# A state attention with two feed-forward nets: first two chunks in four ranges, parts added by the transfer, another opening order

## The chip, the cores and the metric

The kernel runs on one core of a Trainium2 chip. The metric is device microseconds of one execution; the numbers below are the median of several runs and one profiled execution. The engines are TensorE (PE), VectorE (DVE), ScalarE (ACT), GpSimd (POOL) and SyncE (SP), each with an in-order queue of its own; SP mostly issues transfers.

## The reference

Eight batches of an attention between tokens and a small state, then two feed-forward nets over all 4352 rows. The weights are float64, x and state float32.

```python
def _attn_ref(x, state):                       # x (8, 8, 512, 64), state (8, 8, 32, 64)
    scores = scale * np.matmul(x, state.transpose(0, 1, 3, 2))
    a = softmax(scores)                        # written out with max, exp and sum
    xread = np.matmul(a, state)
    scores2 = scale * np.matmul(state, x.transpose(0, 1, 3, 2))
    a2 = softmax(scores2)
    sread = np.matmul(a2, x)
    return np.concatenate([xread, sread], axis=2)

x = attn_out.transpose(0, 2, 1, 3).reshape(B * (S + Ns), 512)
h = np.maximum(x @ w_in, 0.0)                  # w_in 512 x 2048
y = h * h @ w_out                              # w_out 2048 x 512
out = ((y @ w1) * (y @ w2) @ w3) @ w_out2      # 512 x 1024, 512 x 1024, 1024 x 1024, 1024 x 512
```

## The kernel before

Everything is transposed: the 128 partitions hold features, the columns tokens. A *chunk* c is the 512 tokens of one batch (c = 0 to 7); chunk 8 is the 256 state rows of all batches. Products keep fp32 accuracy by splitting each operand into a high and a low half (`split`, L80: ScalarE casts the high half, VectorE subtracts it from the source, line L85, for the low one) and making three passes.

*First net.* For chunk c and each of 16 blocks f of 128 hidden features, `h_tile` (L417) makes six products from `SW` (state times w_in) and `aT` (the softmax), `act_h` (L409) takes relu and square and splits into `ghl`; `y_tile` (L452) makes twelve products of `ghl` with the split w_out (`wo`) into four PSUM banks, one for each d of 128 output features. The main loop (L604 on) runs over (c, f); `y_tile` follows `h_tile` by two tiles. Chunks 0 and 1 alternate in three ranges of f (0 to 4, 4 to 8, 8 to 16, `segs` at L91), so that weights are needed later; each range leaves a partial y per chunk, which is copied by ScalarE (even d) or VectorE (odd d) into one of two `yo` buffers and written to a DRAM scratch of its own by SP. For chunks 2 to 8 there is one range.

*Weights.* They arrive as float64 in pieces of 128 x 512 (three `raw` buffers). `convert64` (L124) makes fp32 by integer arithmetic: VectorE masks the exponent (L136), ScalarE rebases it (L137), VectorE masks the mantissa (L138) and has three more instructions (L141, L144, L147). `make_wout` then has ScalarE cast the high half and GpSimd subtract for the low half (L177). `conv` takes the next conversion of a list and issues the load of the third one after it; `side` and `late` say at which tile i which job is issued. The weights of the second net are converted the same way, later, and parked in DRAM.

*Opening.* SP issues state, x and w_in transfers in program order (L494 on); state goes out as eight small transfers. ScalarE or VectorE copies x of chunk 0 into another layout, GpSimd that of chunks 1 and 2. Then come transposes, scores, softmax, the first `SW` and the first hidden tile.

*Second net.* Pairs of chunks; `load_pair` (L718) reads the parts of y back, and for chunks 0 and 1 GpSimd adds them up.

The order on each engine is set by a scheduler from program order and its own estimates; `issue_after` keeps a job behind a named instruction.

## Time and profile before

| | |
|---|---|
| median of 3 runs | 1298.33 us (1297.55 to 1402.79) |
| the profiled execution | 1299.79 us |
| its span | 1298.0 us |
| busy: TensorE, VectorE, ScalarE, GpSimd | 97%, 62%, 50%, 4% of the span |
| mean granted TensorE clock | 0.988 |

The span is the profiled stretch on the core. A line number in a row is that of kernel.py; a helper such as L85 serves many callers, so the tile's name tells which. In a timeline row stand the start, the duration, engine, line, operation, and in brackets how long the engine had been idle before and what released it. Busy time of TensorE overstates its work, since products are pipelined and their rows overlap.

### The profile page before, as it was taken

Reading aid. Unit: us, or ns where it says so; the run is one execution under the profiler, and the core shown is the slowest. Engines: PE = TensorE matmul, PEld = TensorE weight load, DVE = VectorE, ACT = ScalarE, POOL = GpSimd, SP = SyncE. Lnnn points to the kernel's source line nnn. Section 1 sums busy time; section 2 is a strip of 40 time slices with the busy share of each in tenths; the row PEclk is TensorE's granted clock in tenths of the full one; section 3 lists DMA queues with packets and bytes.
Section 4 is the critical chain, followed back from the end, with each engine's and each line's share of the span. In section 5 each row is a group of like instructions: output and inputs, shape, how many; then the busy total and the mean of one; then the engine's idle time right before and its main releaser. Section 6 shows DMA issues by size and latency. Waiting matters only on the chain.

```text
span 1298.0 us, 16933 instructions
## 1 busy us (share of the span) xinstructions
PE 1255.5 (97%) x6392; PEld 988.4 (76%) x6392; DVE 801.2 (62%) x1428; ACT 651.6 (50%) x1170; POOL 57.4 (4%) x42
## 2 busy tenths in 40 slices
PE   3998999999999999999999999999999999999998
PEld 2575667777777777777789888888888888778877
DVE  6889966767666676733244763747464646566652
ACT  4675765656666575655465542535353542424231
POOL 0122300000000000000000000000510000000000
PEclk8898999999999999999999999999999999999999
DMA  6146626336353633400132432031631425050323
GB/s 210 53 145 199 188 61 179 126 82 186 79 159 97 152 125 81 139 1 28 31 119 82 138 115 75 29 101 43 185 103 44 137 75 158 37 193 19 113 65 98
DMA packets 122962, 137.95 MB, mean 106 GB/s; under 512 B 71424, under 2 KB 75008, under 8 KB 122368
## 3 DMA queue, kind: packets, MB, share of 16 engines
q1 hardware_dynamic: 122880, 136.87, 34.8%
q8 instruction: 50, 0.82, 0.3%
q14 instruction: 32, 0.26, 0.1%
HBM read 93.32 MB, written 43.52 MB: 105 GB/s over the span
## 4 chain that ended last, share of the span: by engine, by line
PE 83%; DVE 8%; DMA 4%; ACT 3%; issue 1%; SPq 0%; POOL 0%; DVEq 0%; ACTq 0%; POOLq 0%
PE y L461 24%; PE po L850 12%; PE qa L769 10%; PE qd L769 6%; PE ps_w L654 3%; PE qc L769 3%; PE qe L769 3%; PE ps_sw L396 2%; PE ab L824 2%; PE ps_r L345 1%; DMA out_dram<-o 1%; DMA x<-in_x_dram 1%; DVE ghl L85 1%; DVE sw L85 1%; DMA yscr<-yo 1%
## 5 line engine op out<-in xcount | busy, mean ns | idle before, releaser
L461 PE MATMUL y<-ghl,wo 128*128 128x512 f32 (+1 forms) x1728 | 408.5, 383 | 8.9 <-ACT yo L470 7.7
L461 PEld LDWEIGHTS y<-ghl,wo 128*128 128x128 f32 x1728 | 309.6, 189 | 101.1 <-ACT r L411 17.6
L85 DVE TENSOR_TENSOR ghl<-r,ghl 128x512 fp32r<-128x512 f32 (+1 forms) x144 | 97.1, 674 | 174.5 <-ACT ghl L84 173.9
L769 PE MATMUL qa<-yq,wq 128*128 128x512 f32 x576 | 146.3, 390 | 1.8 <-ACT s L777 1.8
L769 PEld LDWEIGHTS qa<-yq,wq 128*128 128x128 f32 x576 | 107.6, 188 | 25.9 <-ACT s L777 2.9
L777 ACT COPY s<-qa 128x512 f32<-128x512 f32 x96 | 56.1, 587 | 140.9 <-PE qa L769 128.9
L769 PE MATMUL qd<-yq,wq 128*128 128x512 f32 x384 | 98.3, 390 | 0.0
L850 PE MATMUL po<-w34b,c 128*128 128x512 f32 x408 | 95.8, 391 | 0.3 <-DVE o L859 0.3
L850 PE MATMUL po<-w,c 128*128 128x512 f32 x408 | 95.3, 391 | 0.0
L850 PEld LDWEIGHTS po<-w34b,c 128*128 128x128 f32 x408 | 75.7, 188 | 18.0 <-DVE c L85 1.0
L413 ACT ACTIVATE r<-r 128x512 f32<-128x512 f32 (+1 forms) x144 | 87.5, 608 | 2.9
L850 PEld LDWEIGHTS po<-w,c 128*128 128x128 f32 x408 | 75.6, 188 | 17.4 <-ACT c L84 0.8
L84 ACT CAST ghl<-r 128x512 fp32r<-128x512 f32 (+1 forms) x144 | 86.0, 597 | 5.1 <-PE y L461 1.6
L769 PEld LDWEIGHTS qd<-yq,wq 128*128 128x128 f32 x384 | 71.8, 188 | 15.7 <-ACT s L777 1.0
L137 ACT ACTIVATE ce<-ce,ebias 128x512 int32<-128x512 int32 x72 | 51.7, 722 | 44.3 <-DVE ce L136 44.2
L781 DVE TENSOR_TENSOR s<-qa,s 128x512 f32<-128x512 f32 x32 | 22.1, 692 | 75.5 <-ACT s L777 75.5
L84 ACT CAST c<-s 128x512 fp32r<-128x512 f32 x64 | 39.6, 621 | 35.6 <-DVE s L798 35.1
L727 POOL TENSOR_TENSOR yraw<-yraw,yp 128x512 f32<-128x512 f32 x16 | 21.8, 1362 | 760.5 <-DMA oscr<-o 745.6
L84 ACT CAST yq<-yraw 128x512 fp32r<-128x512 f32 x70 | 42.6, 622 | 24.1 <-DVE yraw L744 15.4
L144 DVE SCALAR_TENSOR_TENSOR ce<-raw,ce 128x512 int32<-128x512 int32 x72 | 50.3, 699 | 4.1 <-ACT ce L137 4.0
L859 DVE TENSOR_TENSOR o<-po,opart 128x512 f32<-128x512 f32 x34 | 23.4, 690 | 46.4 <-PE po L850 35.9
L141 DVE SCALAR_TENSOR_TENSOR cm<-raw,cm 128x512 f32<-128x512 uint32 x72 | 49.9, 693 | 0.8
(549 smaller groups left out, 1862.0 us busy)
## 6 DMA issues: line engine op xcount, KB each, us to landing
raw<-in_moe_w_dram SPq DMA_DIRECT2D x32, 512.0 KB, 4.4
yraw<-yscr SPq DMA_DIRECT2D x56, 256.0 KB, 5.4
raw<-in_moe_w_out_dram SPq DMA_DIRECT2D x24, 512.0 KB, 3.9
yscr<-yo SPq DMA_DIRECT2D x48, 256.0 KB, 2.5
oscr<-o SPq DMA_DIRECT2D x34, 256.0 KB, 2.2
opart<-oscr SPq DMA_DIRECT2D x34, 256.0 KB, 3.2
out_dram<-o SPq DMA_DIRECT2D x32, 256.0 KB, 2.9
raw<-in_moe_w_in_dram SPq DMA_DIRECT2D x12, 512.0 KB, 4.3
```

What stands on the lines that cost most here:

```text
L84: nc.scalar.copy(hi, src)
L85: return nc.vector.tensor_tensor(out=lo, in0=src, in1=f32(hi), op=ALU.subtract)
L137: nc.scalar.activation(e, e, ACTF.Relu, bias=ebias, scale=8.0)
L141: nc.vector.scalar_tensor_tensor(out=f32(m), in0=lw, scalar=2.0**-32, in1=m, op0=ALU.mult, op1=ALU.add)
L144: nc.vector.scalar_tensor_tensor(out=e, in0=hw, scalar=-(2**31), in1=e, op0=ALU.bitwise_and, op1=ALU.bitwise_or)
L396: nc.tensor.matmul(pss[r][k * NS:(k + 1) * NS, cols], stT[rows, b, k, :], win_t[fg][rows, k, cols], start=True, stop=True, tile_position=( ...
L413: nc.scalar.activation(r[:, :n], r[:, :n], ACTF.Square)
L461: nc.tensor.matmul(y_ps[c, d][:, :n], wo_t[f][:, wi, d * P:(d + 1) * P], t[:, gi, :n], start=(f == f0 and k == 0), stop=(f == f1 - 1 and k ...
L654: nc.tensor.matmul(ps, t[:, wi, (j % 4) * P:(j % 4 + 1) * P], wo2_t[j][:, vi, :], start=(j == 0 and k == 0), stop=(j == N1 - 1 and k == 2),)
L769: nc.tensor.matmul(ps, W[w, kt][:, wi, m * P:(m + 1) * P], Y[v, kt][:, vi, :], start=(first and kt == 0 and k == 0), stop=(last and kt == ...
L777: nc.scalar.copy(t, ps)
L850: nc.tensor.matmul(ps, v[:, vi, t * P:(t + 1) * P], w[:, wi, :], start=(m == 0 and k == 0), stop=(m == QM - 1 and k == 2),)
```

## The change

- Chunks 0 and 1 alternate in four ranges of four f each. There is one y scratch for each chunk: the first range is written by SP as before, the later three are added to it in memory by transfers with `accum_op=add`, which GpSimd issues. `load_pair` reads one y and adds nothing.
- `make_wout` no longer uses GpSimd: the split is the common one, on ScalarE and VectorE, and it is put off to the next `conv` (or to the first `y_tile` that needs it).
- `exponents` masks and rebases the exponents of the next piece already while a piece is converted.
- State's first half is issued from ScalarE's queue; both x pieces of chunk 0 go ahead of w_in, x of chunk 1 ahead of state's second half. ScalarE copies x of chunks 1 and 2. Both w_in conversions of the first columns and both softmax halves are issued before the first `aT`; the jobs of tile 0 are issued after the last `aT` of the opening.
- One `conv` for each tile from 7 to 25 (two at 10) in place of 7 to 22 (two at every fourth); the conversions for the second net begin at tile 32 in place of 24.

```diff
-    segs = [[(0, 4), (4, 8), (8, NF)] if c < 2 else [(0, NF)] for c in range(B + 1)]
+    segs = [[(f, f + 4) for f in range(0, NF, 4)] if c < 2 else [(0, NF)] for c in range(B + 1)]
+    y_scr = [dram.tile([P, ND, 512 if c < B else NT9], F32, name=f"yscr{c}") for c in range(B + 1)]
...
+    def exponents(key, t):
+        e = att.tile([P, 512], I32, tag="ce", bufs=2, name="ce")
+        nc.vector.tensor_single_scalar(e, t[:, :, 1], 0x7FF00000, op=ALU.bitwise_and)
+        nc.scalar.activation(e, e, ACTF.Relu, bias=ebias, scale=8.0)
+        exps[key] = e
...
     def make_wout(f):
         w = att.tile([P, 512], F32, tag="cw", bufs=2, name="cw")
         convert64(("wo", f), w)
-        t = wpool.tile([P, 2, DM], F32R, tag="wo", bufs=NF, name=f"wo{f}")
-        nc.scalar.copy(t[:, HI], w)
-        nc.gpsimd.tensor_tensor(out=t[:, LO], in0=w, in1=f32(t[:, HI]), op=ALU.subtract)
-        wo_t[f] = t
+
+        def halves():
+            t = wpool.tile([P, 2, DM], F32R, tag="wo", bufs=NF, name=f"wo{f}")
+            split(t[:, HI], t[:, LO], w)
+            wo_t[f] = t
+
+        open_splits.append(halves)
...
-                nc.sync.dma_start(y_scr[c][part][:, d, :], o[:, :n])
+                if part:
+                    nc.gpsimd.dma_start(y_scr[c][:, d, :], o[:, :n], accum_op=ALU.add)
+                else:
+                    nc.sync.dma_start(y_scr[c][:, d, :], o[:, :n])
...
     load_st(0)
     load_x(0, 0, True)
+    load_x(0, 1, True)
     load_win0(0, 0, True)
-    load_x(0, 1, True)
     make_x(0, 0, nc.vector)
     make_x(0, 1, nc.scalar)
     load_win0(0, 1, True)
-    load_wout(0, True)
     load_win0(1, 0, True)
     load_win0(1, 1, True)
+    load_wout(0, True)
+    for g in range(G):
+        load_x(1, g, True)
     load_st(1)
     for g in range(G):
-        load_x(1, g, True)
-    for g in range(G):
-        make_x(1, g, nc.gpsimd, True)
+        make_x(1, g, nc.scalar, True)
...
     def conv():
+        close_splits()
+        k, k1 = (convs[i] if i < len(convs) else None for i in (pos[1], pos[1] + 1))
         pos[1] += 1
+        if k and k not in exps:
+            exponents(k, raws[k])
+        if k1:
+            exponents(k1, raws[k1])
...
-    for i in range(7, 23):
-        side[i] = [conv] * (2 if i % 4 == 2 else 1)
+    for i in range(7, 26):
+        side[i] = [conv] * (2 if i == 10 else 1)
...
-                nc.sync.dma_start(t[:, n], y_scr[c][0][:, d, :])
-                for part in y_scr[c][1:]:
-                    p = bp.tile([P, 512], F32, tag="pt", bufs=2, name="yp")
-                    nc.sync.dma_start(p, part[:, d, :])
-                    nc.gpsimd.tensor_tensor(out=t[:, n], in0=t[:, n], in1=p, op=ALU.add)
+                nc.sync.dma_start(t[:, n], y_scr[c][:, d, :])
```

The order on SP's queue at the start, before:

```order
L482 DMA st_114<-in_state_dram 32x4x64 x8
L205 DMA x_0_123<-in_x_dram 128x4x256
L119 DMA raw<-in_moe_w_in_dram 128x512 x2
L205 DMA x_1_128<-in_x_dram 128x4x256
L119 DMA raw<-in_moe_w_in_dram 128x512 x2
L121 DMA raw<-in_moe_w_out_dram 128x1024
L119 DMA raw<-in_moe_w_in_dram 128x512 x4
L482 DMA st_145<-in_state_dram 32x4x64 x8
L205 DMA x_0_154<-in_x_dram 128x4x256
L205 DMA x_1_156<-in_x_dram 128x4x256
```

and in the change (x_0_119 and x_1_121 are chunk 0's, x_0_141 and x_1_143 chunk 1's):

```order
L118 DMA raw<-in_moe_w_out_dram 128x1024
L219 DMA x_0_119<-in_x_dram 128x4x256
L219 DMA x_1_121<-in_x_dram 128x4x256
L116 DMA raw<-in_moe_w_in_dram 128x512 x8
L118 DMA raw<-in_moe_w_out_dram 128x1024
L219 DMA x_0_141<-in_x_dram 128x4x256
L219 DMA x_1_143<-in_x_dram 128x4x256
L501 DMA st_145<-in_state_dram 32x4x64 x8
```

State's first half has left this queue, a w_out piece has moved to its head, and x of chunk 1 now stands ahead of the eight small transfers.

VectorE in the first softmax, before, from the maximum of its first half on (`win_210` is w_in, `e_219` the softmax half):

```order
L307 TENSOR_REDUCE mx<-ps_n 128x16
L141 SCALAR_TENSOR_TENSOR cm<-raw,cm 128x512
L308 TENSOR_TENSOR e_219<-ps_n,mx 128x512
L144 SCALAR_TENSOR_TENSOR ce<-raw,ce 128x512
L284 TENSOR_REDUCE nm<-S 128x1
L315 TENSOR_REDUCE sm_229<-e_219 128x16
L147 SCALAR_TENSOR_TENSOR win_210<-cm,ce 128x2x256
L316 TENSOR_SCALAR sm_229<-sm_229 128x16
```

and the same stretch in the change:

```order
L321 TENSOR_REDUCE mx<-ps_n 128x16 x2
L322 TENSOR_TENSOR e_223<-ps_n,mx 128x512
L322 TENSOR_TENSOR e_232<-ps_n,mx 128x512
L329 TENSOR_REDUCE sm_242<-e_223 128x16
L330 TENSOR_SCALAR sm_242<-sm_242 128x16
L331 RECIPROCAL sm_242<-sm_242 128x16
L332 TENSOR_TENSOR e_223<-e_223,sm_242 128x512
L329 TENSOR_REDUCE sm_256<-e_232 128x16
```

The conversions of w_in no longer stand between the steps of the softmax, and the second half (`e_232`) follows the first at once.

VectorE at the end of chunk 0's second part in the change, between the copies of d = 1 (`y_1040`) and d = 3 (`y_1042`), and what follows:

```order
L484 COPY yo<-y_1040 128x512
L125 TENSOR_SCALAR ce<-raw 128x512
L143 TENSOR_SCALAR cm<-raw 128x512
L85 TENSOR_TENSOR ghl<-r,ghl 128x512
L125 TENSOR_SCALAR ce<-raw 128x512
L146 SCALAR_TENSOR_TENSOR cm<-raw,cm 128x512
L149 SCALAR_TENSOR_TENSOR ce<-raw,ce 128x512
L484 COPY yo<-y_1042 128x512
L152 SCALAR_TENSOR_TENSOR cw<-cm,ce 128x512
L85 TENSOR_TENSOR sw_1206<-ps_sw,sw_1206 128x512
L85 TENSOR_TENSOR sw_1209<-ps_sw,sw_1209 128x512
L85 TENSOR_TENSOR wo_1241<-cw,wo_1241 128x512
```

The copy of d = 3 needs the buffer that the transfer of d = 1 empties; the last row is a low half of w_out, which stood on GpSimd before.

## Rows read from the trace of the kernel before

**Rows 1.** The page's first part: busy us, share, instructions.

```profile
PE 1255.5 (97%) x6392; PEld 988.4 (76%) x6392; DVE 801.2 (62%) x1428; ACT 651.6 (50%) x1170; POOL 57.4 (4%) x42
```

**Rows 2.** Stretches: length, busy by engine, PEclk, DMA share, GB/s.

```profile
46.00:100.00 54.00, 53.17 (x318) 35.76 (x316) 47.88 (x99) 39.03 (x72) 12.39 (x7) 1.00 0.38 122
100.00:125.00 25.00, 19.84 (x88) 14.70 (x86) 22.80 (x39) 13.96 (x25) 5.11 (x4) 0.86 0.60 190
125.00:160.00 35.00, 33.04 (x169) 23.93 (x170) 33.70 (x60) 24.54 (x44) 10.46 (x6) 1.00 0.62 189
...
300.00:700.00 400.00, 398.68 (x2179) 306.97 (x2178) 227.52 (x432) 235.35 (x420) 0.00 (x0) 1.00 0.34 94
```

**Rows 3.** Timeline around 160 us: VectorE, ScalarE and TensorE.

```profile
160.17 0.68 DVE L85 TENSOR_TENSOR ghl<-r,ghl 128x512 fp32r<-128x512 f32 x1
...
163.15 0.62 ACT L176 CAST wo<-cw 128x512 fp32r<-128x512 f32 x1 [2.57 <-DVE cw L147]
...
164.31 2.44 PE L396 MATMUL ps_sw<-win,stT 64*32 64x512 f32 x16 [3.46 <-ACT S L279]
```

**Rows 4.** Timeline of VectorE at 134 us.

```profile
134.37 0.68 DVE L144 SCALAR_TENSOR_TENSOR ce<-raw,ce 128x512 int32<-128x512 int32 x1
134.97 0.41 DVE L136 TENSOR_SCALAR ce<-raw 128x512 int32<-128x512 int32 x1
135.31 0.68 DVE L147 SCALAR_TENSOR_TENSOR win<-cm,ce 128x512 f32<-128x512 f32 x1
```

**Rows 5.** Timeline of the opening: TensorE, then VectorE.

```profile
27.24 1.08 PE L328 MATMUL ps_a<-ident,e 128*128 128x128 f32 x4 [7.55 <-DVE rs L291]
...
38.71 0.68 DVE L85 TENSOR_TENSOR aT<-ps_a,aT 128x512 fp32r<-128x512 f32 x1
```

**Rows 6.** Two more stretches, columns as in rows 2.

```profile
10.00:15.00 5.00, 2.13 (x11) 1.73 (x10) 3.29 (x7) 2.84 (x4) 0.00 (x0) 1.00 1.03 385
...
160.00:180.00 20.00, 16.55 (x80) 11.77 (x79) 11.80 (x24) 12.71 (x25) 3.18 (x2) 0.91 0.28 91
```

**Rows 7.** VectorE's groups from 40 to 165 us: busy us, mean ns, idle before.

```profile
L144 DVE SCALAR_TENSOR_TENSOR ce<-raw,ce 128x512 int32<-128x512 int32 x27 | 19.5, 724 | 1.5 <-ACT ce L137 1.4
L141 DVE SCALAR_TENSOR_TENSOR cm<-raw,cm 128x512 f32<-128x512 uint32 x26 | 18.6, 715 | 0.1
L85 DVE TENSOR_TENSOR ghl<-r,ghl 128x512 fp32r<-128x512 f32 x21 | 16.6, 792 | 1.3 <-ACT ghl L84 1.3
L147 DVE SCALAR_TENSOR_TENSOR cw<-cm,ce 128x512 f32<-128x512 f32 x15 | 13.1, 871 | 1.4 <-POOL wo L177 1.2
...
L147 DVE SCALAR_TENSOR_TENSOR win<-cm,ce 128x512 f32<-128x512 f32 x12 | 9.1, 761 | 0.0
```

**Rows 8.** The same groups from 210 to 700 us.

```profile
L85 DVE TENSOR_TENSOR ghl<-r,ghl 128x512 fp32r<-128x512 f32 x101 | 69.5, 688 | 160.3 <-ACT ghl L84 160.3
...
L147 DVE SCALAR_TENSOR_TENSOR cw<-cm,ce 128x512 f32<-128x512 f32 x37 | 25.4, 686 | 0.5
L144 DVE SCALAR_TENSOR_TENSOR ce<-raw,ce 128x512 int32<-128x512 int32 x37 | 25.3, 684 | 0.1
```

**Rows 9.** VectorE's waits from 40 to 165 us: total, times, longest.

```profile
DVE ce L144 <- ACT ce L137: 1.4, 1, 1.4
...
DVE yo L468 <- DMA yscr<-yo: 1.2, 2, 1.0
DVE cw L147 <- POOL wo L177: 1.2, 1, 1.2
```

**Rows 10.** Transfers: writes of a part (60 to 240 us), reads of one.

```profile
DMA to landing us min/median/max: 2.0/3.1/5.8
...
yp<-yscr SPq DMA_DIRECT2D x16, 256.0 KB, 3.3
```

**Rows 11.** The chain at 370 us: start, us, what.

```profile
370.04 1.36 PE ph__3529 L425 x6
371.40 2.72 PE y L461 x12
```

49 lines of the change are left out of this document (26 added, 23 removed).

## The prediction

> **What bounds it now.** I read the page's busy times first: TensorE is busy 97% of the span [rows 1], so what can be gained is the time in which it waits or computes at half clock. The table of stretches says where that is. From 300 to 700 us it is busy 398.7 of 400 us and VectorE 227.5: nothing to gain there. Between 46 and 160 us it is the other way round: VectorE is busy 47.9 of 54, 22.8 of 25 and 33.7 of 35 us, so it stands idle for 9.6 us of 114 [rows 2]. The weights arrive as 64-bit floats and VectorE turns each 512 KB piece into fp32 by five instructions; while that lasts, VectorE sets the pace and TensorE waits for it, often inside rows that count as busy. Where the lateness shows, the wait is named after another engine: at 163.15 ScalarE starts a cast that had waited 2.57 us for VectorE's `cw`; the two copies of `S` queue behind that cast, and TensorE waits 3.46 us for `S` [rows 3].
>
> So the account is kept on VectorE: its time to a fixed point is the work that stands ahead of that point in its own order, plus its waits, plus what its instructions take too long. A long instruction (128x512, 0.68 us) costs 0.60 us from start to start, a short one (0.41 us) 0.34 us [rows 4]. The point is the low half of the 21st hidden tile (`ghl`, L85), which starts at 160.17 [rows 3]. Counted in the two programs' orders, 157 long and 68 short instructions stand ahead of it before (94.2 + 23.1 = 117.3 us) and 160 long and 62 short in the change (96.0 + 21.1 = 117.1 us); the tiny ones are 34 in both. That is no accident of counting: twelve low halves of w_out come over from GpSimd (12 x 0.60 = 7.2 us), and three conversions of 2.5 us each have moved behind the point, since four ranges want the last weights later. The work is equal, so only waits and slow instructions change.
>
> **The change part by part.**
>
> *Opening, -4.0 us on VectorE.* Before, TensorE stands 7.55 us before the first transpose of the softmax at 27.24, and the low half of chunk 0's second `aT` starts at 38.71 [rows 5], ending near 39.3, with 27 long and 14 short instructions done by then (21.0 us): VectorE is 18.3 us late. In the change both x pieces of chunk 0 come before w_in, the state goes out from ScalarE's queue beside them, and both softmax halves run ahead of the second half of w_in. Ahead of x for chunk 1 lie 5.25 MB (state 0.25, two w_out pieces 1.0, x 1.0, w_in 2.0, x itself 1.0); the opening has reached 385 GB/s [rows 6], 13.6 us for all of it; with some 2 us to the first byte and 1.3 us to issue and land the last, its two pieces land near 15.6 and 16.9 us. I estimate ScalarE's two copies of them to end at 16.6 and 19.0, the second exponential behind them at 19.7, the second normalised half at 21.2, and the same low half of `aT` at 25.7, with 16 long and 6 short instructions done (11.6 us): 14.1 us late. That is 4.2 us less; I keep 4.0, for four tiny instructions fewer. TensorE's first hidden tile comes some 14 us earlier, but from there VectorE paces it. Bounds: 0 if chunk 1's x lands 4 us later, since ScalarE's exponential queues behind its copy; 7 if it lands 3 us sooner.
>
> *GpSimd does no arithmetic any more, -7.8 us.* Beside it VectorE's instructions were slow. From 40 to 165 us against 210 to 700 us, where GpSimd is idle, the means are: `ghl` 792 for 688 ns (21 of them, 2.2 us), `cw` 871 for 686 (15, 2.8 us), the same step on `win` 761 for 686 (12, 0.9 us), L144 724 for 684 (27, 1.1 us) and its like L141 715 (26, 0.8 us) [rows 7, 8]. Sum 7.8 us. Bounds: 7.8 is the measured excess of five groups; it falls to 3.9 if GpSimd, which now prepares the accumulating transfers in this stage, disturbs half as much by that.
>
> *Exponents one conversion ahead, -2.6 us.* VectorE waited 1.4 us for ScalarE's exponent and 1.2 us for GpSimd to free `cw` [rows 9]. Both causes go. A raw piece must now have landed one step sooner; yet in the order the work between the freeing of a raw buffer and the reading of its next content stays at 4 us at least and about 6 mostly in both programs, so the waits for raw data stay as they are.
>
> *Accumulating transfers, +2.2 us ahead of the point.* 24 transfers of 256 KB now add in memory, issued from GpSimd's queue. None is in the trace. The nearest row is the plain write of the same tile, 2.0 at least, 3.1 in the median, 5.8 at most; a read of the same part takes 3.3 [rows 10]. One that has to read and then write takes 3.1 at least and 3.3 + 3.1 = 6.4 if one follows the other; I take 4.5, nearer to the write, since reading and writing overlap along the lines of a transfer. Only two `yo` buffers exist, so the copy of d = 3 on VectorE waits for the transfer of d = 1. Between the two copies VectorE has three long and three short instructions, 2.8 us; it stands still for 4.5 - 2.8 = 1.7 us, and the conversions, `ghl` and casts behind it with it. Two such part ends lie ahead of the point: 3.4 us, less the 1.2 us that `yo` cost before [rows 9]. Bounds: -1.2 and +6.
>
> What the Trainium skill says of such transfers (DMA: Bandwidth & Descriptors, section "Anatomy of one DMA") would make it shorter: 2.0 us fixed plus bytes over 436 GB/s, an estimate of 2.6 us for these. By it VectorE would not wait at all and the forecast would be 1279 us. No run here shows it, and its fit is not for accumulation.
>
> *Behind the point, +1.4 us.* Between the 21st and the 24th `ghl` the change has 24 long and 7 short instructions, 16.8 us, where TensorE needs three tiles of 1.36 + 2.72 us [rows 11] and about 1.5 us of attention and `sw` products: 13.7. It loses 3.1 us, and one more part end costs VectorE 1.7 us: 4.8. Before, the same stretch lost the 3.45 us that TensorE is idle from 160 to 180 and 1.8 us by a granted clock of 0.91 [rows 6]: 5.2 us. So this is nearly even (-0.4). Three part ends are left after that, where VectorE has time again and TensorE itself is the one that would wait: it wants the bank of d = 2 again 5.4 us after a part's last tile begins (2.72 + 1.36 + 1.36), and the buffer needed for emptying it was filled at about 2.2 us: a cover of 3.2 us, or 4.3 where `sw` products stand between. Of 4.5 us that leaves 0.2 to 1.3; I take 0.6 for each, 1.8 in all, and so +1.4.
>
> *At no cost:* the 16 additions and 16 reads that fall away in the pair (0, 1) lie beside a TensorE that never waits for them; the stretch from 300 us on shows the same [rows 2]. ScalarE gets chunk 2's two x copies, about 1 us each, and would block if x were late; its margin is several tiles.
>
> **Sum.** -4.0 - 7.8 - 2.6 + 2.2 + 1.4 = -10.8 us. The profiled execution took 1299.8 us (span 1298.0); that gives 1289.0. The median of the runs, 1298.33, lies 1.5 us lower, so I say 1287, rounded down.
>
> **The rivals.**
>
> *A, VectorE lets go.* If the new order also removes the rest of VectorE's idle time (9.6 - 2.6 - 1.2 = 5.8 us) and part ends cost nothing (3.4 + 1.7 + 1.8), TensorE runs almost unhindered: 1287 - 12.7, about 1274, and with the upper bound of the opening, 3 us more, 1271. For it: the scheduler spreads the conversions evenly. Against it: idle time on a saturated VectorE came from many small causes that the change doesn't touch.
>
> *B, slow accumulation, the other side.* Each us above 4.5 costs 1 us at each of the six part ends, at three through VectorE and at three on TensorE itself: 6 us per us. The gain of 10.8 is gone at 6.3 us, where the kernel becomes slower than before; 6.4 us, read after write, gives 1298, 7 us give 1302. Slower by over 2% would need 10.7 us. For it: a plain write took up to 5.8 us [rows 10]. Against it: those stood behind loads in SP's queue, which these don't. The Trainium skill has a rule on this side too (SBUF — State Buffer, section "Who interferes with whom"): GpSimd cannot write descriptors while VectorE runs an instruction in its two-port mode. No run here shows it; VectorE's instructions of 0.41 us could hold it up, but none for long.
>
> *C, the opening doesn't get earlier.* If x for chunk 1 lands at 21 us or later, ScalarE's queue holds back the second softmax as GpSimd's did not: 1291 to 1295.
>
> **How the numbers follow.** The forecast has 0.53, with a range of its own of 1280 to 1294; A 0.23; B 0.16; C 0.08. The range 1268 to 1300 leaves out a tail of A and the upper half of B. About 2% is what a measurement of this kernel can tell from no change: faster than 1272.4 is most of A's lower half and a tail of the forecast, 0.16; slower than 1324.3 only a B of over 10 us, 0.04; the rest, 0.80, is within.
>
> **What would show it.** Right: the first hidden tile done near 26 us (41 before), no `ghl` or `cw` above 0.7 us, the 21st `ghl` near 148, VectorE still over 90% busy from 46 to 145 us. The accumulating transfers' time to landing decides between A and B. Wrong: VectorE with idle time in the middle while TensorE still waits, or waits for raw data that take over on VectorE.

## The result

The changed kernel takes 1307.84 us (median of 4 runs, 1306.15 to 1307.96) where the kernel before takes 1298.3: a ratio of 1.0072, 95% interval 1.0053 to 1.0092. It is 0.7% slower. The forecast was 1287, with 1300 as the upper end. The profiled execution took 1307.75 us, its span 1305.7.

The page's first part and the head of its chain, after (before: [rows 1]):

```profile
PE 1259.8 (96%) x6392; PEld 990.0 (76%) x6392; DVE 797.4 (61%) x1448; ACT 657.0 (50%) x1178; POOL 21.6 (2%) x30
...
PE 80%; issue 12%; ACT 3%; DVE 2%; DMA 2%; POOL 1%; ACTq 0%; SPq 0%; POOLq 0%; DVEq 0%
```

GpSimd has gone from 57.4 to 21.6 us and VectorE has lost a little, yet the span is longer. Where, the stretches say (columns as in [rows 2]):

```profile
46.00:100.00 54.00, 52.57 (x301) 36.06 (x294) 50.54 (x109) 38.71 (x70) 0.00 (x0) 1.00 0.41 132
100.00:125.00 25.00, 19.76 (x89) 14.24 (x88) 19.62 (x37) 15.54 (x25) 3.61 (x4) 0.96 0.77 206
125.00:160.00 35.00, 31.74 (x158) 23.33 (x158) 28.27 (x55) 21.52 (x38) 3.48 (x4) 0.93 0.66 147
160.00:210.00 50.00, 44.27 (x232) 32.15 (x231) 30.72 (x63) 28.07 (x53) 6.93 (x8) 0.93 0.67 115
210.00:250.00 40.00, 37.36 (x177) 25.18 (x177) 24.24 (x49) 22.10 (x39) 6.93 (x8) 0.96 0.64 110
300.00:700.00 400.00, 398.58 (x2145) 305.40 (x2145) 238.40 (x456) 237.53 (x420) 0.00 (x0) 1.00 0.37 106
```

Up to 100 us VectorE does more than before (50.5 of 54 us, 47.9 before). From 46 to 145 us it was to be busy over 90%; it is busy 84.7 of 99 us (before 90.5), and from 100 to 160 us 47.9 of 60 us (before 56.5). TensorE loses with it: 51.5 of 60 us from 100 to 160, then 81.6 of 90 from 160 to 250 us (before 52.9 and 85.6). From 300 us on nothing has changed. The mean granted clock is below full speed in all four stretches from 100 to 250 us. GpSimd's column is one row of 0.9 to 1.2 us for each accumulating transfer, four for each end of a part.

One such end, the first, in the timeline (the bracket is the idle time before and what ended it):

```profile
113.53 0.57 ACT L486 COPY yo<-y 128x512 f32<-128x512 f32 x1
...
114.42 1.01 POOL L488 DMA_DIRECT2D yscr<-yo  x1 [113.12 <-ACT yo L486]
...
114.87 0.68 DVE L484 COPY yo<-y 128x512 f32<-128x512 f32 x1
...
115.86 0.87 POOL L488 DMA_DIRECT2D yscr<-yo  x1 [0.43 <-DVE yo L484]
...
121.51 0.58 ACT L486 COPY yo<-y 128x512 f32<-128x512 f32 x1 [4.87 <-DMA yscr<-yo]
...
122.15 1.09 PE L477 MATMUL y<-ghl,wo 128*128 128x512 f32 x3 [4.51 <-ACT yo L486]
...
122.80 0.69 DVE L484 COPY yo<-y 128x512 f32<-128x512 f32 x1 [3.34 <-DMA yscr<-yo]
```

ScalarE's first copy ends at 114.10, and its buffer can be filled again at 121.51: 7.4 us. VectorE's ends at 115.55 and the next begins at 122.80: 7.25 us. The prediction had 4.5 us here. ScalarE stands 4.87 us before the copy of d = 2, TensorE 4.51 us behind it for the bank, and VectorE 3.34 us before d = 3 with the conversion behind it.

Waits for the two buffers up to 260 us, and the transfers (before: 1.2 us up to 165 us [rows 9]; plain writes 3.1 us [rows 10]):

```profile
DVE yo L484 <- DMA yscr<-yo: 19.3, 7, 5.0
ACT yo L486 <- DMA yscr<-yo: 16.1, 7, 4.9
```

```profile
yscr<-yo SPq DMA_DIRECT2D x32, 256.0 KB, 2.6
...
yscr<-yo POOLq DMA_DIRECT2D x24, 256.0 KB, 5.4
```

The time to landing counts from the start of GpSimd's row, so that the 0.9 to 1.2 us of this row lie inside it; only 0.3 us, from the end of the copy to the row, come on top. The 5.4 us are the median of 24. At this first end, where the transfer engines are busiest (0.77 from 100 to 125 us), the first two transfers take 7.1 and 6.9 us. Over the six ends a buffer of the first two copies is filled again 4.8 to 7.6 us after it was filled, 6.2 in the mean.

What was promised of VectorE's speed is there. Its groups from 40 to 165 us (before: [rows 7]):

```profile
L149 DVE SCALAR_TENSOR_TENSOR ce<-raw,ce 128x512 int32<-128x512 int32 x26 | 17.7, 682 | 0.0
L146 DVE SCALAR_TENSOR_TENSOR cm<-raw,cm 128x512 f32<-128x512 uint32 x25 | 17.1, 685 | 0.0
L85 DVE TENSOR_TENSOR ghl<-r,ghl 128x512 fp32r<-128x512 f32 x20 | 13.7, 685 | 4.4 <-ACT ghl L84 4.4
...
L152 DVE SCALAR_TENSOR_TENSOR cw<-cm,ce 128x512 f32<-128x512 f32 x14 | 9.6, 684 | 0.0
```

Every long instruction is at 682 to 685 ns (724, 715, 792 and 871 before), and the waits for exponents and for `cw` are gone.

How the lead was lost is seen best tile by tile. This table gives, worked out from the timelines, when TensorE begins a hidden tile, for the profiled execution of five kernels, as us against the kernel before (which begins tile 10 at 96.0, 14 at 122.2, 36 at 241.3). Tiles 0 to 31 are those of the first two chunks. The last four columns are experiments that follow.

```
tile   after  plain parts  same, GpSimd queue  accumulation alone  conversions alone
10      -3.4      -3.6           -0.7               -0.7                -3.6
14     -10.5     -10.6           -7.6               -0.1                -6.7
15      -4.2      -9.6           -1.0               +3.0                -8.2
21      +0.1      -8.8           -0.7              +10.4                -9.8
24      +1.4     -12.0           -0.8               +7.5               -14.9
36      +8.6     -11.5           -0.6              +15.5               -15.0
48      +8.7     -11.4           -0.5              +15.5               -15.0
```

Up to tile 14 the changed kernel leads by 10.5 us. The first accumulating end takes 6.3 of them, and by tile 36 it is 8.6 us late; there it stays.

### The profile page after: what moved, and what is told of

Its sections match the earlier page's. It is cut to its first block, busy times and chain, and to the rows that moved or that the text cites. A ratio compares the mean times of both kernels' runs of the same rounds, so it can differ in the third digit from the quotient of the medians.

```text
span 1305.7 us, 16892 instructions
## 1 busy us (share of the span) xinstructions
PE 1259.8 (96%) x6392; PEld 990.0 (76%) x6392; DVE 797.4 (61%) x1448; ACT 657.0 (50%) x1178; POOL 21.6 (2%) x30
## 4 chain that ended last, share of the span: by engine, by line
PE 80%; issue 12%; ACT 3%; DVE 2%; DMA 2%; POOL 1%; ACTq 0%; SPq 0%; POOLq 0%; DVEq 0%
PE y L477 21%; PE po L872 14%; PE qa L791 10%; PE qd L791 7%; PE qc L791 3%; PE ps_w L680 3%; PE qe L791 3%; PE ab L846 2%; PE ps_sw L410 2%; POOL yscr L488 1%; PE ps_r L359 1%; DMA yscr<-yo 1%; PE ps_s L287 1%; PE ps_w L665 1%; DVE sw L85 0%
## 5 line engine op out<-in xcount | busy, mean ns | idle before, releaser
L477 PE MATMUL y<-ghl,wo 128*128 128x512 f32 (+1 forms) x1728 | 410.4, 383 | 17.2 <-ACT yo L486 11.6
L84 ACT CAST yq<-yraw 128x512 fp32r<-128x512 f32 x70 | 42.6, 622 | 23.3 <-DVE yraw L766 15.4
L791 PE MATMUL qc<-yq,wq 128*128 128x512 f32 x192 | 49.5, 390 | 0.0
```

The costliest lines, as they stand in the source:

```text
L84: nc.scalar.copy(hi, src)
L477: nc.tensor.matmul(y_ps[c, d][:, :n], wo_t[f][:, wi, d * P:(d + 1) * P], t[:, gi, :n], start=(f == f0 and k == 0), stop=(f == f1 - 1 and k ...
L791: nc.tensor.matmul(ps, W[w, kt][:, wi, m * P:(m + 1) * P], Y[v, kt][:, vi, :], start=(first and kt == 0 and k == 0), stop=(last and kt == ...
```

## The experiments

Times are medians; "before" is the kernel before, run on the same chip with the experiment (1298.4 to 1299.0). What a kernel gives against it is the difference of the two medians.

### Is it the accumulation?

**Plain parts.** Four ranges stay; each part has its own place, and the pair (0, 1) adds them.

```diff
-                if part:
-                    nc.gpsimd.dma_start(y_scr[c][:, d, :], o[:, :n], accum_op=ALU.add)
-                else:
-                    nc.sync.dma_start(y_scr[c][:, d, :], o[:, :n])
+                nc.sync.dma_start(y_scr[c][part][:, d, :], o[:, :n])
...
+                for part in y_scr[c][1:]:
+                    p = bp.tile([P, 512], F32, tag="pt", bufs=2, name="yp")
+                    nc.sync.dma_start(p, part[:, d, :])
+                    nc.gpsimd.tensor_tensor(out=t[:, n], in0=t[:, n], in1=p, op=ALU.add)
```

> The changed kernel, but each of the four parts of chunks 0 and 1 is written plainly from SyncE's queue to its own place in memory, and the pair (0, 1) reads and adds the four parts on GpSimd, as the kernel before does with three. Everything else (opening, conversions, four ranges, order) stays as changed. Theory L (the accumulating transfer frees a yo buffer only 7.3 us after the copy ends, where 4.5 was assumed, and only two buffers exist): a plain write frees it about 3 us after it is issued, so the six part ends lose about 3 us less each, 18 in all: 1286 to 1293. Rival R (four ranges have two more part ends than three, and these cost what they cost however the parts are written): 1303 to 1309. Rival Q (plain writes stand in SyncE's queue behind loads that wait for a raw buffer, one was issued 8 us after its copy before): 1296 to 1303.

1306.86 us, ratio 1.006 (1.0039 to 1.0082): by its time alone, rival R. The trace says otherwise. The waits for `yo` up to 260 us fall from 35.4 to 6.5 us, and the kernel is 11.4 us ahead of the one before from tile 36 on (table). It loses 13.6 us at another place, ahead of the pair (0, 1). The waits for `yo`, then the stretches ahead of the pair, then the waits from 860 to 965 us:

```profile
ACT yo L489 <- DMA yscr<-yo: 3.8, 4, 1.4
...
DVE yo L487 <- DMA yscr<-yo: 2.7, 4, 1.1
```

```profile
900.00:920.00 20.00, 20.00 (x90) 16.53 (x90) 7.58 (x10) 6.01 (x11) 10.77 (x9) 1.00 0.67 206
920.00:940.00 20.00, 17.67 (x77) 13.99 (x75) 12.54 (x15) 7.58 (x14) 12.55 (x10) 1.00 0.40 113
940.00:960.00 20.00, 10.54 (x33) 7.89 (x34) 5.95 (x10) 4.60 (x9) 7.78 (x7) 0.66 0.27 78
```

```profile
ACT yq L84 <- POOL yraw L753: 18.0, 3, 10.8
...
PE qa L795 <- ACT s L803: 9.9, 1, 9.9
```

Four parts need 24 reads and 24 additions of 1.3 us on GpSimd: 31.4 us of work, with 22.2 us of waits for the reads between; the 16 additions of the kernel before (21.8 us) keep nobody waiting. ScalarE's in-order queue stops at the cast of a piece that isn't summed yet, for up to 10.8 us; behind it stands a copy out of PSUM, and for that TensorE waits 9.9 us and then computes at a granted clock of 0.66. So the adding transfers do save something here: about 14 us that plain writes in four parts would lose. The profiled execution was the fastest of the four (1302.36 us): the two places explain its 2.2 us against the kernel before, and 6 of the 8.2 us between the medians are in no trace.

**The queue apart from the addition.** Plain parts, issued from GpSimd's queue.

```diff
-                nc.sync.dma_start(y_scr[c][part][:, d, :], o[:, :n])
+                (nc.gpsimd if part else nc.sync).dma_start(y_scr[c][part][:, d, :], o[:, :n])
```

> As the kernel with plain parts, but parts 1 to 3 are issued from GpSimd's queue, as the accumulating ones were; the pair (0, 1) reads and adds four parts. It separates the addition in the transfer from the queue that issues it. Theory L in the form that the addition makes it long: landing near 2.6 to 3.1 us, as from SyncE's queue, and 1283 to 1292. Rival P (GpSimd's queue is the slow part: the 0.9 us of issuing and its own way to the transfer engines): landing stays above 5 us and the time within 3 us of 1307.8.

1313.75 us, 1.0115 (1.01 to 1.013), the same loss at the pair included; even without it (13.6 us) the time would be near 1300, above what theory L had said. Landing is 3.1 us, as theory L had it, but the waits for `yo` are 18.6 us:

```profile
yscr<-yo POOLq DMA_DIRECT2D x24, 256.0 KB, 3.1
```

```profile
ACT yo L489 <- DMA yscr<-yo: 10.4, 6, 4.7
...
DVE yo L487 <- DMA yscr<-yo: 8.2, 6, 2.3
```

So both the queue and the addition cost something. At tile 10 this kernel is already 2.9 us behind the plain parts from SyncE, before its first write from GpSimd's queue (117 us); so the count begins at tile 14. From there to tile 36 plain parts from SyncE gain 0.9 us, those from GpSimd lose 7.0, and the changed kernel loses 19.1: of 20.0 us 7.9 go with the queue and 12.1 with the addition (one execution each; between the medians of the two plain kernels lie 6.9).

The queue's share is not in the landing: from 60 to 260 us that is 2.9 us in the median from SyncE's queue and 3.1 from GpSimd's. Most of it falls at the first end, where this kernel loses 6.6 us, the changed one 6.3 and plain parts from SyncE 1.0 (tiles 14 to 15). The first two writes take nearly as long there in all three: 6.9 and 6.1 us, 7.1 and 6.9, 5.9 and 5.1. What differs is the order that the scheduler gave: with writes from GpSimd's queue ScalarE has four instructions between the copies of d = 0 and d = 2 and then stands, with writes from SyncE's it has seven (two casts of `sw` and an exponent more), and TensorE takes the next hidden tile first. That the order is the cause is argued; no run has one order with both queues. Behind the first end plain parts from GpSimd lose nothing (-1.0 to -0.6), and the adding ones 12.8 us.

The Trainium skill (DMA: Bandwidth & Descriptors, section "Anatomy of one DMA — SWDGE (gpsimd) path") gives 2.0 us plus bytes over 436 GB/s, an estimate of 2.6 us; the plain transfer from this queue takes 3.1 here and the adding one 5.4, and the measurement decides.

**Accumulation alone.** The kernel before, with its three parts added by the transfer.

```diff
-                nc.sync.dma_start(y_scr[c][part][:, d, :], o[:, :n])
+                if part:
+                    nc.gpsimd.dma_start(y_scr[c][:, d, :], o[:, :n], accum_op=ALU.add)
+                else:
+                    nc.sync.dma_start(y_scr[c][:, d, :], o[:, :n])
```

> The kernel before with one part of the change alone: its three parts of chunks 0 and 1 are added in memory by the transfer, issued from GpSimd's queue, and the pair (0, 1) reads one sum; opening, conversions and ranges stay as before. Theory L: four accumulating part ends, each 3 us dearer than a plain one: 1306 to 1313. Rival R (accumulation costs nothing, the two more ends do): 1297 to 1300.

1313.03 us, 1.0108 (1.0092 to 1.0125): 14.4 us slower for four accumulating ends, 3.6 us each, at the upper end of theory L. They too hold the queue's effect on the order: at the third of these ends ScalarE has two instructions between its two copies, before fourteen. TensorE's waits for the emptied bank show it (up to 260 us; before 6.5 us in the same stretch):

```profile
PE y L458 <- ACT yo L467: 16.5, 5, 4.7
...
ACT yo L467 <- DMA yscr<-yo: 14.0, 4, 3.9
...
DVE yo L465 <- DMA yscr<-yo: 12.7, 4, 4.3
```

**A third buffer.** The changed kernel, with a buffer of its own for d = 2.

```diff
-        m = att.tile([P, 512], I32, tag="cm", bufs=2, name="cm")
+        m = att.tile([P, 512], I32, tag="cm", bufs=1, name="cm")
...
+                if c < 2 and d == 2:
+                    o = att.tile([P, 512], F32, tag="yo2", bufs=1, name="yo")
+                else:
+                    o = pa.tile([P, 512], F32, tag="yo", bufs=2, name="yo")
```

> The changed kernel with a third buffer for the emptied banks of chunks 0 and 1: the copy of d = 2 gets one of its own, so only d = 3 still waits for the transfer of d = 0. Room for it comes from the second cm buffer, which only VectorE writes and reads. Transfers stay as they are. Theory L (the wait for the buffer is the loss): the 4 to 5 us that ScalarE and TensorE stand before the copy of d = 2 at each of six ends go, some 2 us each come back at d = 3: 1290 to 1299. Rival R (the two more part ends themselves, or the traffic of the accumulating transfers beside the loads): 1303 to 1309.

1303.35 us, 1.0034 (1.0021 to 1.0047): 4.5 us better than the change, less than expected and just inside rival R's span. ScalarE no longer waits for `yo`, VectorE still does for 15.6 us (19.3 in the change), and the transfers land later, 6.1 us in the median. The buffer is a part of the loss; a third one doesn't cure it, and the single `cm` buffer may cost something that this run doesn't separate.

### What is the rest worth without it?

**Adding later, in memory.** Plain parts from SyncE; parts 1 to 3 are added to part 0 by transfers from memory to memory, and the pair reads one sum.

```diff
...
+    def fold(c, part, d):
+        return lambda: nc.gpsimd.dma_start(y_scr[c][0][:, d, :], y_scr[c][part][:, d, :], accum_op=ALU.add)
+    for n, (part, c, d) in enumerate((p, c, d) for p in range(1, 4) for c in range(2) for d in range(ND)):
+        side[40 + 3 * n].append(fold(c, part, d))
```

> As the kernel with plain parts up to the end of the first two chunks; but the parts are no longer read and added for the pair (0, 1). Instead parts 1 to 3 are added to part 0 later, in the stretch of the other chunks, by 24 accumulating transfers from memory to memory on GpSimd's queue, spread over every third tile from the 40th on, with no buffer in SBUF. The pair reads one sum. Theory: plain parts reach 300 us 11.4 us ahead of the kernel before and lose 13.6 us later, because 24 reads and 24 additions of 1.3 us on GpSimd are too many for the time ahead of the pair (0, 1), where TensorE stands for some 12 us between 925 and 955 us; with the sum made earlier the lead stays: 1285 to 1289. Rival: the loss behind 300 us is another (conversions of the later weights, or their order): 1296 or more, with TensorE idle elsewhere.

1292.86 us, 0.9953 (0.9938 to 0.9968): 6.1 us faster than before, 15 us faster than the change. The loss ahead of the pair is gone. Less is left than expected, and the folds do not wait for their tile: nothing holds GpSimd's queue, and the first go out at 120 us.

```profile
120.24 1.84 POOL L592 DMA_DIRECT2D yscr<-yscr  x2 [118.93 <-DMA yscr<-yo]
```

**Really later.** A tiny instruction on VectorE, and one on GpSimd that waits for it, hold back six groups of four folds.

```diff
+            g = [pa.tile([P, 1], F32, tag=f"gate{k}", bufs=1, name="gate") for k in range(2)]
+            nc.vector.memset(g[0], 0.0)
+            go = nc.gpsimd.tensor_copy(g[1], g[0])
+            with tc.issue_after(go.ins):
...
+        side[44 + 12 * n].append(fold(n))
```

> As the kernel that folds its plain parts later, but really later: there the 24 transfers from memory to memory ran from 120 us on, as soon as two parts had landed, and the transfer engines were 83% busy between 125 and 160 us where they were some 60% busy without them. Here six groups of four are held until VectorE has passed the tiles 44, 56, ... 104 (a tiny instruction on VectorE and one on GpSimd ahead of each group). Theory: beside the weights' loads the early folds cost what the kernel with plain parts was ahead (11.4 us at 300 us, against 6.3): 1286 to 1290. Rival: its lead was the luck of one execution, as its times from 1302 to 1309 suggest: 1291 to 1294.

1297.81 us, 0.999 (0.9981 to 0.9999): neither. At tile 48 it is 9.8 us ahead, better than the early folds' 6.3. It gives 3.1 us back between tiles 82 and 84 (see the four ranges below), and in the second net the matmuls of three groups take 3 to 4 ns longer and wait for nothing, at the full clock. So the two tiles of 4 bytes were made 128 bytes wide, and nothing else:

```diff
-            g = [pa.tile([P, 1], F32, tag=f"gate{k}", bufs=1, name="gate") for k in range(2)]
+            g = [pa.tile([P, 32], F32, tag=f"gate{k}", bufs=1, name="gate")[:, :1] for k in range(2)]
```

> As the kernel with late folds, but its two tiny tiles are 128 bytes wide instead of 4. In the three kernels with the 4-byte tiles TensorE's matmuls take 394 ns instead of 391 in the products of the second layer (437 in 100 us instead of 441), with no wait. Theory M (the 4-byte tiles shift the addresses of the tiles behind them, and TensorE reads those more slowly): matmuls of 391 ns again, and 1290 to 1293. Rival (the slower matmuls come from something else, such as what the folds leave in memory): 1296 to 1299.

1291.84 us, 0.9949 (0.9935 to 0.9964): 6 us back. One of the three groups of matmuls from 800 to 1200 us, with 4 bytes:

```profile
L886 PE MATMUL po<-w,c 128*128 128x512 f32 x384 | 91.6, 394 | 0.0
```

and with 128 bytes:

```profile
L886 PE MATMUL po<-w,c 128*128 128x512 f32 x384 | 89.7, 391 | 0.0
```

Late folds are worth 1 us over early ones by the medians, with intervals that overlap: the padded kernel is 8.3 us ahead at tile 48, the early folds 6.3, but it gives 3.3 us back between tiles 82 and 84. The four runs that follow stand on kernels of this family.

**Exponents not ahead** (on the late folds with 4-byte tiles).

```diff
-        if k1:
-            exponents(k1, raws[k1])
```

> As the kernel with late folds, but the exponents are no longer computed one conversion ahead: each conversion begins with its own mask and its own step on ScalarE, as before. The prediction's term for the step ahead is -2.6 us: 2 to 4 us slower than the kernel with late folds. Rival, that the wait for the exponent was covered by the other work of VectorE: within 1 us of it.

1295.19 us, 0.9974 (0.9965 to 0.9984), 2.6 us faster than with the step ahead (1297.81, 0.9981 to 0.9999): the term of -2.6 us has the opposite sign here, though the intervals just touch. On three ranges it pays (below), so it depends on what stands around it.

**Parts of d = 0 and 2 from ScalarE's queue** (same base).

```diff
+                (nc.sync if c >= 2 or d % 2 else nc.scalar).dma_start(y_scr[c][part][:, d, :], o[:, :n])
```

> As the kernel with late folds, but the parts of d = 0 and 2 are written from ScalarE's queue, right behind the copy that ScalarE itself makes, and no longer from SyncE's, where a write can stand behind a load that waits for its raw buffer. With plain writes from SyncE's queue the waits for a yo buffer are 6.5 us in all, and TensorE waits about as long for the copies. If these go: 2 to 5 us faster than the kernel with late folds. Rival (issuing costs ScalarE as much as it saves): within 1 us.

1298.52 us, 1.0003 (0.9993 to 1.0013), 0.7 us above its base: nothing gained.

**A third buffer for plain parts** (early folds, the edit of the third buffer above).

> As the kernel that folds its plain parts later, with the third buffer for the emptied banks of chunks 0 and 1 (copy of d = 2). Waits for yo are 6.5 us in all with plain writes and two buffers, and only half of these are seen by TensorE: 1 to 4 us below the two-buffer version, 1282 to 1287. If the part ends are bound by the copies and not by the buffers: the same within 1 us.

1295.57 us, 0.9975 (0.9964 to 0.9985): 2.7 us slower than with two buffers (0.9938 to 0.9968). With plain writes a third buffer gains nothing; that the single `cm` buffer is what costs is argued.

**Low halves back on GpSimd** (early folds).

```diff
-            split(t[:, HI], t[:, LO], w)
+            nc.scalar.copy(t[:, HI], w)
+            nc.gpsimd.tensor_tensor(out=t[:, LO], in0=w, in1=f32(t[:, HI]), op=ALU.subtract)
```

> As the kernel that folds its plain parts later, but the low halves of w_out are subtracted on GpSimd again, as in the kernel before; everything else stays. Twelve instructions of 0.60 us go from VectorE to GpSimd up to the 21st tile, 7.2 us, and GpSimd's arithmetic beside VectorE makes VectorE's instructions longer again. The prediction put this excess at 7.8 us: by that 0 to 3 us slower than with the halves on VectorE, 1286 to 1291. Rival, that GpSimd's arithmetic costs VectorE little and the twelve halves are simply spared: 4 to 7 us faster, 1279 to 1283.

1292.91 us, 0.9952 (0.9937 to 0.9967), the same as with the halves on VectorE (1292.86). VectorE's instructions are slow again, as the prediction said: from 40 to 165 us by some 7 us in all, 3.1 of them in the 27 exponent masks (535 ns for 419 in the kernel with early folds), the rest in these two groups (681 and 685 ns there). The twelve spared instructions of 0.60 us are worth as much:

```profile
L152 DVE SCALAR_TENSOR_TENSOR ce<-raw,ce 128x512 int32<-128x512 int32 x27 | 21.0, 781 | 0.0
L85 DVE TENSOR_TENSOR ghl<-r,ghl 128x512 fp32r<-128x512 f32 x20 | 14.8, 739 | 3.8 <-ACT ghl L84 3.6
```

### Each part alone

**The opening alone**, on the kernel before; of the change's diff the lines for the first loads, the state's queue, `make_x`, `soft1a` and the first tile's gate, and no others.

```diff
+    load_x(0, 1, True)
     load_win0(0, 0, True)
-    load_x(0, 1, True)
...
+    make_win0(0, 1)
     s1a[0]()
+    s1a[1]()
...
-    s1a[1]()
-    make_win0(0, 1)
...
-    at[1]()
+    first = at[1]()
```

> The kernel before with the new opening alone: both x pieces of chunk 0 ahead of w_in, the state from ScalarE's queue, x of chunk 1 copied by ScalarE, both softmax halves ahead of the second half of w_in, the first tile's jobs held until the last aT. Ranges, conversions and parts as before. The prediction's term for it is -4.0 us: 1293 to 1296. Rival C (TensorE's start is earlier but VectorE, paced by the conversions, gives it all back): 1297 to 1300. Rival, that the whole lead of 9.4 us at the first hidden tile stays: 1288 to 1291.

1295.05 us, 0.9975 (0.9966 to 0.9985): -4.0 us, the forecast's own number.

**The conversions alone**, on the kernel before: exponents ahead, low halves of w_out on VectorE and split one conversion later; the old opening, three plain ranges.

```diff
-        nc.scalar.copy(t[:, HI], w)
-        nc.gpsimd.tensor_tensor(out=t[:, LO], in0=w, in1=f32(t[:, HI]), op=ALU.subtract)
+        def halves():
...
+            split(t[:, HI], t[:, LO], w)
...
+        close_splits()
...
+        if k1:
+            exponents(k1, raws[k1])
```

> The kernel before with the change's conversions alone: the low halves of w_out on VectorE, split after the conversion of the next piece has been opened, and exponents one conversion ahead; opening, three ranges and their parts and the order of the conversions as before. The prediction has -7.8 us for GpSimd's arithmetic (its adding in the pair aside) and -2.6 us for the exponents, and 12 x 0.60 = 7.2 us more work on VectorE, which the change as a whole makes good by moving three conversions: -3.2 us here, 1294 to 1297. If the contention is not worth its measured excess, it is 1 to 5 us slower than before: 1300 to 1304.

1284.71 us, 0.9901 (0.9879 to 0.9923): -14.2 us, far more than expected. TensorE's waits go almost entirely between 100 and 180 us, and it has the full clock in the opening, where the kernel before has 0.68 and 0.66 (stretches as in [rows 2]):

```profile
15.00:31.60 16.60, 7.75 (x39) 3.39 (x39) 13.98 (x30) 7.95 (x15) 2.41 (x2) 1.00 0.61 200
31.60:46.00 14.40, 12.47 (x67) 7.82 (x66) 12.04 (x28) 8.59 (x18) 0.00 (x0) 1.00 0.12 38
100.00:113.00 13.00, 10.83 (x51) 6.61 (x50) 11.90 (x22) 7.01 (x12) 1.10 (x1) 1.00 0.65 218
160.00:180.00 20.00, 20.00 (x116) 15.32 (x116) 17.22 (x36) 14.46 (x27) 0.00 (x0) 1.00 0.40 93
```

One stop of the kernel before shows how so much can come of it. Around 100 us three of VectorE's instructions, each beside a row of GpSimd, take 1.5 to 1.8 us in place of 0.7. ScalarE's exponent waits 3.34 us for them, the copy of d = 2 stands behind it in ScalarE's queue, and TensorE waits 4.67 us for that copy, at a mean granted clock of 0.74 from 100 to 113 us:

```profile
96.83 1.76 DVE L147 SCALAR_TENSOR_TENSOR cw<-cm,ce 128x512 f32<-128x512 f32 x1 [1.19 <-POOL wo L177]
...
99.57 1.77 DVE L85 TENSOR_TENSOR ghl<-r,ghl 128x512 fp32r<-128x512 f32 x1
...
101.26 1.52 DVE L141 SCALAR_TENSOR_TENSOR cm<-raw,cm 128x512 f32<-128x512 uint32 x1
...
103.75 0.72 ACT L137 ACTIVATE ce<-ce,ebias 128x512 int32<-128x512 int32 x1 [3.34 <-DVE ce L136]
...
104.38 0.57 ACT L470 COPY yo<-y 128x512 f32<-128x512 f32 x1
...
105.00 2.93 PE L461 MATMUL y<-ghl,wo 128*128 128x512 f32 x6 [4.67 <-ACT yo L470]
```

With the conversions this stop is gone, and their lead grows from 3.6 to 11.0 us between tiles 10 and 12; 4.3 of that are lost again by tile 14. The wait for `S` at 164 us [rows 3] is gone too: the lead is 9.8 us at tile 21 and 14.9 at tile 24.

**Halves of it.** First without the exponents ahead, then with the low halves on GpSimd; each takes one of the two edits just shown back.

> The kernel before with the low halves of w_out on VectorE, each split after the next conversion has been opened; exponents not ahead, opening and ranges as before. It divides the 14.2 us of the conversions. By the prediction: -7.8 for the contention, +7.2 for the work, so 1297 to 1300, and the gain would have to come from the exponents. Rival: taking ScalarE's cast and GpSimd's low half out of the chain of a conversion (VectorE waited for GpSimd to free cw, ScalarE's copies queued behind its cast) is what pays: 1286 to 1291.

1291.45 us, 0.9943 (0.9926 to 0.996): -7.3.

> As the kernel before with the change's conversions alone, but with the low halves of w_out on GpSimd as before: what is left is the exponent one conversion ahead and the cast of w_out one conversion later. By the prediction's -2.6 us and the wait for cw: 1294 to 1297. Rival (the late cast no longer holds up ScalarE's queue, and that is the whole gain): 1285 to 1290.

1292.87 us, 0.9957 (0.9942 to 0.9971): -5.8. The two make 13.1 of the 14.2 us. Each pays more than its term (-0.6 net for the low halves, -2.6 for the exponents). Both also bring ScalarE's cast of w_out one conversion later, behind work that it held up before. The traces show what that shares: in all three kernels TensorE is busy 20.0 of 20 us from 160 to 180 us, and between tiles 21 and 24 each gains 4.1 to 5.4 us on the kernel before. The rest doesn't follow from the late cast, which no run has alone; only the kernels with the low halves on VectorE lose the stop at 105 us.

**Conversions and opening together**, three ranges: the two edits just shown, on the kernel before.

> The kernel before with the change's conversions and its opening, but with three ranges, plain parts, and the conversions in the old order: everything of the change except the four ranges and the accumulating transfers. Alone the conversions gave 14.2 us and the opening 4.0. Theory F (both are worth what they are alone, and what the change loses beside the accumulation it loses by the four ranges): 1279 to 1283. Rival G (both give the same waits of TensorE back, so they don't add; the four ranges are innocent): 1284 to 1289.

1287.19 us, 0.9912 (0.9898 to 0.9927): -11.5. They don't add; on top of the conversions the opening costs 2.5 us, which alone is within the noise of the two (the clearer case follows with four ranges). Its first stretches, to be read beside those of the conversions alone:

```profile
15.00:31.60 16.60, 11.21 (x62) 6.10 (x62) 10.92 (x22) 7.83 (x13) 0.00 (x0) 0.71 0.51 160
31.60:46.00 14.40, 10.33 (x59) 6.70 (x58) 11.69 (x28) 11.27 (x23) 0.00 (x0) 0.74 0.01 2
```

VectorE has done 22.6 us of work from 15 to 46 us, with the old opening 26.0, and TensorE is back at a granted clock of 0.71 to 0.74. Why the clock falls with one opening and not with the other, the runs don't say.

**Four ranges on the conversions**, old opening, plain parts, padded late folds.

```diff
-    segs = [[(0, 4), (4, 8), (8, NF)] if c < 2 else [(0, NF)] for c in range(B + 1)]
+    segs = [[(f, f + 4) for f in range(0, NF, 4)] if c < 2 else [(0, NF)] for c in range(B + 1)]
...
```

> The four ranges and the order of conversions that goes with them, on top of the change's conversions, but with the old opening; parts plain, folded late in memory (padded tiles). Beside the kernel with the conversions alone (1284.7) it differs by the ranges only, beside the padded late folds (1291.8) by the opening only. Theory F (the ranges cost some 5 us, the new opening on top of the conversions some 2 us): 1288 to 1291. Rival (the ranges cost nothing and the new opening all of it): 1284 to 1286. Rival (the new opening is needed by the four ranges): 1293 or more.

1286.91 us, 0.9911 (0.9894 to 0.9927): -11.5. That is 2.2 to 2.7 us more than the conversions alone, with intervals that overlap. The trace doesn't put it on the ranges: from tile 36 to tile 80 this kernel is 14.2 us ahead and the conversions alone 15.0. It loses 4.0 us between tiles 82 and 84, where four late folds meet the loads and the plain writes of a later chunk's end (the transfer engines are busy 0.93 and more from 430 to 450 us); TensorE waits for the bank, and its mean granted clock is 0.74 from 450 to 455 us:

```profile
452.04 1.38 PE L480 MATMUL y<-ghl,wo 128*128 128x512 f32 x3 [2.67 <-ACT yo L489]
```

All five kernels with late folds lose something there (0.9 to 5.0 us), the kernels without them nothing; that the folds are the cause is argued from that. The new opening costs 4.6 to 4.9 us more (the padded late folds: 1291.84, -6.9), and here the intervals lie apart.

**The x copies alone.** The conversions alone, and the x copies of chunks 1 and 2 on ScalarE.

```diff
-        make_x(1, g, nc.gpsimd, True)
+        make_x(1, g, nc.scalar, True)
...
-                side[i].append(lambda b=b, g=g: (load_x(b, g), make_x(b, g)))
+                side[i].append(lambda b=b, g=g: (load_x(b, g), make_x(b, g, nc.scalar)))
```

> The kernel before with the change's conversions alone, and in addition the x copies of chunks 1 and 2 on ScalarE, so that GpSimd computes nothing up to the last pair. Four copies of 128x1024 leave GpSimd. If what is left of contention is worth anything: 1282 to 1284. If ScalarE's in-order queue blocks behind a copy whose x is late, as it does in the new opening: 1286 to 1289.

1283.05 us, 0.9885 (0.987 to 0.99): -15.4, the fastest kernel of the study, though its interval overlaps with that of the conversions alone. So the opening's loss doesn't come from these copies alone. From 100 to 113 us TensorE is now busy throughout:

```profile
15.00:31.60 16.60, 8.59 (x45) 3.67 (x47) 13.98 (x31) 9.73 (x17) 0.00 (x0) 1.00 0.61 208
...
100.00:113.00 13.00, 13.00 (x69) 9.79 (x68) 12.19 (x23) 9.27 (x17) 0.00 (x0) 1.00 0.80 260
```

### The account

Each step on top of the one before, from the medians against the kernel before, and beside it the same from the start of tile 48 in the traces (one execution each):

```
                                               medians                 tile 48
conversions                                   -14.2   (to 1284.7)       -15.0
four ranges, parts added later in memory       +2.7   (-11.5)            +0.8
new opening                                    +4.6   (-6.9)             +5.9
parts added by the transfer at each end       +16.4   (+9.5, the change) +17.0
```

The two kernels in the middle lose 3.3 to 4.0 us more behind tile 48, by their late folds; the medians hold that, the last column doesn't. The last step takes plain writes and late folds away and puts accumulating ends in their place.

## Why the prediction was wrong

**Accumulating transfers: the step that failed.** "I take 4.5, nearer to the write." From issue to landing it takes 5.4 us in the median, between the two values that were weighed, 4.5 and 6.4; the buffer, which also waits 0.3 us for GpSimd's row, is away for 6.2 us in the mean of the six ends and 7.3 at the first. The three terms for accumulating ends (3.4, 1.7 and 1.8) make 6.9 us; measured against plain ends they are 16.4, 2.7 for each end, and so 9.5 us more than forecast. Its own rival B prices that well: each us above 4.5 costs 6 us, so 6.2 us cost 10. By this alone the kernel would have come out near 1297, about as before; that it is slower takes the opening too.

Two things stood in the way of a higher value. That reading and writing overlap was taken as a reason for the low one, and no row showed it. And against B stood that these transfers don't queue behind loads as SyncE's do. At the first end that gained nothing: beside the loads the adding transfers take 7.1 and 6.9 us, and plain writes from SyncE's queue 5.1 to 7.4 in three kernels. The addition shows behind it, where the first two transfers of an end take 4.4 to 7.0 us and plain ones from SyncE's queue 2.0 to 4.8. What the prediction didn't see at all is that another queue also changes the scheduler's order around the copies (the first end costs 6.6 us with plain writes from GpSimd and 1.0 from SyncE; that the order makes the difference is argued).

**Opening: right number alone, wrong sign in company.** The sign named was that the second `aT`'s low half starts at 25.7 with VectorE 14.1 us late. It starts at 29.93:

```profile
23.84 1.08 PE L342 MATMUL ps_a<-ident,e 128*128 128x128 f32 x4 [4.19 <-DVE e L332]
...
29.93 0.69 DVE L85 TENSOR_TENSOR aT<-ps_a,aT 128x512 fp32r<-128x512 f32 x1 [0.80 <-ACT aT L84]
```

With the same 11.6 us of work VectorE is 19.0 us late, where it was 18.3 before [rows 5]: by the prediction's own account the opening gave nothing. Chunk 1's x lands at 19.1 and 21.5 us, not at 15.6 and 16.9, and ScalarE's two copies of it end at 20.1 and 22.7, not at 16.6 and 19.0. That is about the bound that was named for no gain (x 4 us later). A small part is the sum itself: 5.25 MB, counted in units of 2^20 bytes, take 14.3 us at 385 GB/s and not 13.6. That the opening alone still gives 4.0 us comes from elsewhere: the number was luck, and confirms nothing. On top of the conversions the opening costs 4.6 to 4.9 us with four ranges, 8.6 us off the forecast; why, beyond the lower clock in its first stretches, is open. The first hidden tile was to be done near 26 us: TensorE begins it at 26.4 (31.6 before), but ScalarE starts `ghl`'s cast at 33.7 (43.1 before).

**GpSimd's arithmetic: right.** No `ghl` or `cw` is above 0.7 us, and giving the halves back to GpSimd brings slow instructions back and changes the time by nothing: contention and spared work cancel, some 7 us against 7.2, with 7.8 against 7.2 in the prediction. That holds with four ranges. With three, the halves on VectorE are worth 8.2 us (1284.71 against 1292.87): a slow instruction that stands ahead of a copy, as at 105 us, can cost TensorE more than its own excess; that this makes the 8.2 us is argued. The Trainium skill (SBUF — State Buffer, section "Who interferes with whom") says that VectorE's operations with two inputs from SBUF contend with GpSimd's reads; the rows agree, with 781 ns beside GpSimd's arithmetic and 682 without for the same instruction.

**Conversions: mechanism right, too small.** Alone they give 14.2 us, with 7.2 us more work on VectorE. The prediction kept its account on VectorE; the lateness passed through ScalarE's queue. One such stop it knew and priced behind the point (the wait for `S` of [rows 3], 5.2 us with the clock). The other, TensorE's 4.67 us at 105 us, had no term of its own.

**Four ranges: hardly a cost.** The ends were priced for their transfers alone, and the order of conversions counted as equal work. In the trace they cost 0.8 us up to tile 80; the 2.2 to 2.7 us of the medians are within the noise and hold the late folds too.

**Part additions "at no cost": right for the 16.** They keep GpSimd busy for 21.8 us and are hidden; 24, which plain parts in four ranges would need, take 31.4 us and cost about 14. So the change's adding transfers spared more than the prediction gave them.

In sum, against the forecast's -10.8 us the change came out at +9.5: 9.5 us from the accumulating ends, 8.6 from the opening, 6.0 from the ranges and what was to be regained behind the 21st tile (-3.3 expected with the `yo` waits saved, +2.7 measured), less 3.8 that the conversions gave in excess. How the last two divide depends on where the 7.2 us of halves on VectorE and the three conversions that moved behind the point are counted; here to neither. Of the signs that were named, the time to landing, 5.4 us, lies above the forecast's 4.5 and below B's break-even of 6.3; the buffer's 6.2 lies just at it. The 21st `ghl`, due near 148, came at 158.3, with plain parts from SyncE at 149.3.
